# Seven half-size products for eight: the last layer of an attention and MLP kernel by Strassen's method

## The chip, the cores and the metric

The kernel runs on one core of a Trainium2 chip. The metric is the device time of one execution in microseconds (us); the median of several runs is compared. Engines are called PE (TensorE, matmuls), DVE (VectorE), ACT (ScalarE), POOL (GpSimd) and SP (SyncE, which issues transfers).

## The reference

Eight batches of attention with a relative position bias, then an MLP on all 8 x 576 = 4608 rows:

```python
scores = q @ k.T / sqrt(64) + bias           # per batch and head: 576 x 576
attn   = softmax(scores)
x      = (attn @ v), heads side by side      # 4608 x 512
h      = x @ w_in                            # 4608 x 2048
s      = sin(alpha * h)
g      = h + s * s / (alpha + 1e-9)
out    = g @ w_out                           # 4608 x 512
```

## The kernel before

The attention goes batch by batch (t = 0 to 7), the MLP in nine blocks (b = 0 to 8) of 512 rows. All matmuls have f16 operands and write f32 into PSUM, the tile `pb` of eight banks of 512 columns each.

The attention of a batch makes scores (k stationary, q moving, runs of six matmuls of 512 columns), exponentials on ACT into `u`, a multiplication by exp(bias) (`m2r`, `mhr`) on DVE for the part near the diagonal, and attention times v (`av`: nine matmuls of 65 or 130 columns for 128 rows and a pair of heads). DVE divides by the row sums (`rd`, `xn`), and a transposing transfer, or TensorE and a copy, puts the result into `xT`.

A block of the MLP has two stages. `plan_moe_in`: for each of 16 tiles f of 128 hidden columns, four matmuls of 512 columns into a bank `h`; ACT takes the sine, ACT or DVE squares it, and DVE forms g (`gg`), which lies in SBUF as `g[:, f, 512]`, f16. `plan_mo`: for each of the four groups of 128 rows, 16 matmuls of 512 columns (g stationary, `w_out16` moving) add up in one bank; a copy by DVE or ACT into `outs` and a transfer on SP's queue end it. The two banks for these products are 7 and 6 in turn.

The order of each engine's instructions is made when the kernel is built, by `Plan.run`: tasks with a cost per engine, dependencies, a priority and buffers, of which always the one that can start first is emitted. Output products are marked `fill`: they are put between a batch's score runs (`QUOTA` of them at most while the scores run). So the output products of block b mostly run inside the attention of batch b + 1. Engines work in order; the waits between them (semaphores) are put in from the order of emission and from the tiles that instructions touch.

Loads on POOL's queue: `stage_kq(t)` copies k and q of a batch, cast to f16, into DRAM (576 KB each), from where SP's transposing transfers fetch them; `load_v16(t)` loads v. In the kernel before, the first g of block b (1 to 6) triggers `load_v16(b + 1)` and `stage_kq(b + 2)`; a separate task stages batch 2.

Of the kernel before, what the change touches and what calls it, by code (L numbers as in the profile page):

```python
# [13 lines left out]
ALU = mybir.AluOpType  # L14
# [21 lines left out]
NBUF = {"ut": 2, "u": 2, "g": 2, "s16": 3, "sq": 3, "outs": 5, "xn": 6}  # L36
PAIRS = ((0, 1), (2, 3), (4, 5))
BANKS = {"h": (0, 1, 2, 3, 4, 5), "av": (6, 7), "mo": (7, 6)}


class Task:
    def __init__(self, engs, emit, deps, pri, nb=0.0):
        self.engs, self.emit, self.deps, self.pri, self.nb = engs, emit, list(deps), pri, nb
        self.allocs = []
        self.marks = []
        self.offs = None
        self.s_only = self.fill = False
        self.pad = ()
        self.end = self.eng = None
# [12 lines left out]
class Plan:  # L62


    def __init__(self):
        self.tasks = []
        self.sin = self.in_qk = False
# [26 lines left out]
    def pick(self, b, taken):  # L94
        sets = PAIRS if b.tag == "sc" else [(k,) for k in BANKS[b.tag]]
        best = None
        for ks in sets:
            if any(k in taken for k in ks):
                continue
            fr = [self.bank_free(k) for k in ks]  # L100
            if any(x is None for x in fr):
                continue
            if best is None or max(fr) < best[0]:
                best = (max(fr), ks)
        return best

    def ready(self, t):
        r = t.nb
        for d in t.after:
# [6 lines left out]
        n_ring, banks = {}, set()  # L116
        t.got = []
        for i, b in enumerate(t.allocs):
            if b.tag in NBUF:
                ring, n = self.rings[b.tag], NBUF[b.tag]  # L120
                k = n_ring[b.tag] = n_ring.get(b.tag, -1) + 1
                if len(ring) + k >= n:
                    for x in ring[k - n].users:
                        if x.end is None:
                            return None
                        r = max(r, x.end)
                continue
            got = self.pick(b, banks)
            if got is None:
                return None  # L130
            banks.update(got[1])
            t.got.append((b, got[1]))
            r = max(r, got[0] - (t.offs[i] if t.offs else 0.0))
        return r
# [14 lines left out]
    def run(self, t0):  # L149
        free = {e: t0 for e in ("PE", "ACT", "DVE", "POOL", "SP")}  # L150
        todo = list(self.tasks)
        while todo:
# [21 lines left out]
            for e, c in cands.items():  # L174
                if not c:
                    continue
                s0 = min(x[0] for x in c)
                st, t = min(((x[0], x[1]) for x in c if x[0] <= s0 + SLACK[e]),
                            key=lambda x: (x[1].pri, x[0]))
                fin = st + t.engs[e]  # L180
                if best is None or (st, fin) < best[:2]:
                    best = (st, fin, e, t)
# [18 lines left out]
            for x, off in t.marks:  # L201
                x.end, x.eng = st + off + LAT[e], e
# [7 lines left out]
WINDOW = 700  # L210
# [5 lines left out]
SPLIT = {0: 3, 1: 3}  # L216
# [24 lines left out]
SQ = {"ACT": 0.52, "DVE": 0.38}  # L241
# [9 lines left out]
AV_PRI = 400  # L251
# [18 lines left out]
def kernel(  # L270
# [61 lines left out]
    zz = sgl.tile([128, 512], F16, name="zz")  # L332
# [6 lines left out]
    phi_x = sgl.tile([NB, EW + 2 * NB], F16, name="phi_sb")  # L339
    phi_sb, less_last = phi_x[:, 0:EW], phi_x[:, EW : EW + 2 * NB].bitcast(F32)  # L340
    e_sb = sgl.tile([H, EW], F16, name="e_sb")
    alphaN = sgl.tile([NF, 128], F32, name="alphaN")
# [33 lines left out]
    def new_sq():  # L376
        return tp.tile([128, DM], F16, name="sq", tag="sq", bufs=NBUF["sq"])

# [279 lines left out]
    def plan_unit(t, p, kind, c, u, ub, done, gate, base):  # L658
# [73 lines left out]
        elif kind == "A":  # L732
            lo, hi = max(0, 128 * c - 128), min(512, 128 * c + 256)

            def bd(e):
                io = u.v[:, y, 0:8, lo:hi].rearrange("p (z c) q -> p z c q", z=2)[:, :, c]
                x0 = lo - 128 * c + 128
                nc.vector.tensor_tensor(  # L738
                    out=io, in0=io, in1=m2[:, 2 * p : 2 * p + 2, x0 : x0 + hi - lo], op=ALU.mult
                )  # L740

            engs = {"DVE": 0.1 + (hi - lo) / 960.0}
# [60 lines left out]
    def plan_att(t, gates, gate):  # L803
# [5 lines left out]
        runs = (A[0:3], [(0, "C", 0)], A[3:6], A[6:9], A[9:12], [(2, "C", 0)], A[12:15],  # L809
                A[15:] + [(0, "B", 0), (2, "B", 0)], [(0, "X", 0)])  # L810
        bases = [PB + 700 * i for i in range(len(runs))]
        exps, head, seen = [], [], set()
        for i, units in enumerate(runs):
# [18 lines left out]
            tl = plan_tail(t - 1, base) if i == 0 and t > 1 else None  # L832

            def run(e, i=i, made=made, tl=tl, fresh=fresh):
                if i == 0:
                    plan.in_qk, plan.used = True, 0
                    plan.quota = QUOTA1 if t == 1 else QUOTA
# [3 lines left out]
                if i == len(runs) - 1:  # L841
                    plan.in_qk = False
                for x in made:
                    x[2](e)
                if tl:
# [6 lines left out]
                         use=use + ([tl[3]] if tl else []))  # L852
            m.offs = ([d] if tl else []) + [0.0] * len(new) + [
                0.1 + 0.2185 * k - GUARD[x[1]] * (k > 1) for k, x in enumerate(units)]
            m.marks = [(x[1], o) for x, o in zip(made, ends)] + ([(tl[4], d + D_TAIL)] if tl else [])
            head = [m]
            exps += [x[3] for x in made]
        for p in range(NP):
            plan_av(t, [(p, 128 * i) for i in range(3)], *us[p // 2], done, bases[(2, 3, 5, 7)[p]],
                    p < (2, NP - 1)[t > 1])  # L860
# [5 lines left out]
        return exps  # L866
# [22 lines left out]
    def plan_tail(t, base):  # L889
# [23 lines left out]
        def norm(e):  # L913
            xn.v = new_xn()
            norm_av(av.v, xn.v)

        x = plan.add({"DVE": 0.67}, norm, [mark], base, new=[xb], use=[ab])
# [40 lines left out]
    def plan_av(t, parts, u, ub, done, base, dma):  # L958
# [42 lines left out]
        x = plan.add({"DVE": (0.4 if t else 0.29) + 128 * nq / 960.0}, norm, prev, base + (NORM_PRI if t else NORM0),  # L1001
# [42 lines left out]
    def plan_moe_in(b, tbl):  # L1044
# [5 lines left out]
        for f in range(NF):  # L1050
# [3 lines left out]
            def mm(e, js, f=f, h=h, hb=hb):  # L1054
# [4 lines left out]
                for y, a, n in ((0, x0, m), (m, 0, 512 - m)):  # L1059
                    if n == 0:  # L1060
                        continue
                    for j in js:
                        full(h.v[:, y : y + n], w_in16[:, j, 128 * f : 128 * f + 128],
                             xT[:, j, a : a + n], j == 0, j == 3)
# [14 lines left out]
            def gg(e, f=f, h=h, sq=sq):  # L1079
# [12 lines left out]
            pri = PB + 10000 + 1000 * (b - (PB // 1000000)) + 10 * f  # L1092
            nb = T_W[f // 8] if b == 0 else 0.0
            m = None
            if f < SPLIT.get(b, 0):
                m = plan.add({"PE": 3 * t_pe(512)}, lambda e, mm=mm: mm(e, range(NP - 1)), xs[1], pri - PRI_S,
                             nb=nb, new=[hb])
# [3 lines left out]
                         use=[hb] if m else [])  # L1101
# [10 lines left out]
    mo_last = []  # L1112

    def plan_mo(b, a):

        for c0, c1 in ((0, 384), (384, DM)) if (b, a) == (T, 3) else ((0, DM),):
            mb, ob, m = Buf("mo"), Buf("outs"), Cell()
            n = c1 - c0
            for f in range(NF):
# [13 lines left out]
                mo_last[0].fill = True  # L1133

# [8 lines left out]
            y.s_only = True  # L1143

# [11 lines left out]
    for t in range(T):  # L1156
        PB = 1000000 * t

        if t > 0:
            gate = [plan.add({"ACT": D_TBL}, lambda e: set_table(EXP_SET), sins, PB)]  # L1160
        exps = []
        for p in range(NP - 1) if t == 0 else ():
            for kq in range(2):
                tr[(0, p + 1, kq)] = plan_tr(0, p + 1, kq, (150, 650, 5)[p], T_PAIR[p][kq])
        if t == 0:
            for g in range(2):
                exps += plan_att0(g, pe_gate, gate)
        else:
            exps += plan_att(t, pe_gate, gate)
            if t == 1:  # L1170
                exps += plan_late(PB + LATE, gate)
        if t == 0:
# [3 lines left out]
            plan.add({"POOL": 5.0}, lambda e: stage_kq(2), [], 10090,  # L1176
# [4 lines left out]
        def turn_in(e, t=t):  # L1181
            load_kqT(t + 1)
            load_kt(t + 1)

        tbl = [plan.add({"ACT": D_TBL}, swap, exps, PB)]
        if 1 <= t < T - 1:
            plan.add({"SP": 5.5}, turn_in, [], PB + 9000, after=tbl + [
                x for tt, _, _, x in xdone if tt == t and "SP" in x.engs])
# [3 lines left out]
        for b in [t] if t < T - 1 else [t, t + 1]:  # L1192
            m, s_ = plan_moe_in(b, tbl)
            sins += s_
        pe_gate = [m]
        for b in [t] if t < T - 1 else [t, t + 1]:
            for a in range(4):
                plan_mo(b, a)
# [31 lines left out]
```

## Time and profile before

Three runs took 373.75, 372.87 and 376.17 us; the profiled execution spans 374.9 us.

| engine | busy us | share of the span | instructions |
|---|---|---|---|
| PE | 368.2 | 98% | 3576 |
| DVE | 257.8 | 69% | 559 |
| ACT | 315.7 | 84% | 431 |
| POOL | 91.9 | 25% | 133 |

The costliest groups that the change touches, from the list of groups by shape:

| line, engine, what | count | busy us | mean ns |
|---|---|---|---|
| L457 PE output products, 512 columns | 560 | 135.5 | 379 |
| L457 PE first-layer products, 512 columns | 448 | 99.2 | 379 |
| L1082 DVE g, 128x512 | 144 | 101.3 | 744 |
| L1077 DVE sq, 128x512 | 75 | 30.9 | 422 |
| L539 DVE copy of an output, 128x512 | 25 | 17.2 | 686 |
| L953 DVE xn, 128x256 and 128x384 | 29, 28 | 12.3, 15.6 | 425, 557 |
| L738 DVE masked u, 128x512 and 128x768 | 64, 64 | 26.8, 35.9 | 423, 563 |

A middle block takes about 39.55 us from one attention's end to the next (194.96 to 234.51): PE busy 39.55, ACT 36.58, DVE 29.50. A row of a timeline gives start, length, engine, line, output <- inputs, tile size, shape, how many were merged, and in brackets the idle time before it with the engine that ended it. A matmul's length contains its way through the array, so lengths overlap; starts tell the pace.

### The profile page before, as it was taken

To read this page: it belongs to the slowest core of one execution; us is meant where nothing else is said; L and a number is where in the kernel's file an instruction comes from. 1 tells how busy PE (TensorE), PEld (TensorE's weight loads), DVE (VectorE), ACT (ScalarE), POOL (GpSimd) and SP (SyncE) were. 2 spreads that over 40 slices of the span, in tenths; PEclk is the share of its full clock that TensorE was granted. 3 is DMA by queue.
4 is the path that set the end of the run, shared out by engine and by line. 5 is a ranking of instruction groups with operands and counts; after the bars stand their busy time and mean duration, and the time that the engine had idled before them with its cause. 6 is when DMAs were issued, how large, how long until landed. Compare 5 with 4: busy or idle time off the path is not lost.

```text
span 374.9 us, 8925 instructions
## 1 busy us (share of the span) xinstructions
PE 368.2 (98%) x3576; PEld 197.4 (53%) x3576; DVE 257.8 (69%) x559; ACT 315.7 (84%) x431; POOL 91.9 (25%) x133
## 2 busy tenths in 40 slices
PE   8999999999999999999999999999999999999996
PEld 3455454644455455684564455444576455444443
DVE  3496976759676967597758867786759675879000
ACT  2787989979997999899989999799979997999211
POOL 7368270037000640055002800090006000000000
PEclk9999999999999999999999999999999999999999
DMA  9969999369922998199917992699249121000112
GB/s 168 201 113 192 200 173 160 83 112 112 133 64 62 151 143 123 48 160 137 133 48 134 125 168 58 122 88 187 59 111 118 65 58 47 7 27 5 73 69 85
DMA packets 149114, 40.49 MB, mean 108 GB/s; under 512 B 137080, under 2 KB 143568, under 8 KB 149072
## 3 DMA queue, kind: packets, MB, share of 16 engines
q0 software_dynamic: 96032, 17.67, 58.3%
q1 hardware_dynamic: 52864, 22.16, 24.6%
q8 instruction: 28, 0.46, 0.5%
q10 hardware_dynamic: 176, 0.09, 0.1%
q14 instruction: 14, 0.11, 0.1%
HBM read 37.73 MB, written 16.56 MB: 145 GB/s over the span
## 4 chain that ended last, share of the span: by engine, by line
PE 95%; ACT 3%; DVE 1%; issue 0%; ACTq 0%
PE pb L457 92%; ACT u L707 3%; PE pb L556 2%; PE pb L1024 1%; PE pb L550 0%; DVE xn L953 0%; DVE u L738 0%; DVE qT L539 0%; DVE zz L508 0%; ACT outs L537 0%; ACT xT L537 0%; DVE rd L952 0%; PE pb L646 0%; PE pb L934 0%; ACTq L537 0%
## 5 line engine op out<-in xcount | busy, mean ns | idle before, releaser
L707 ACT ACTIVATE u<-pb 128x1024 f16<-128x1024 f32 (+1 forms) x146 | 137.4, 1017 | 11.9 <-PE pb L457 10.5
L457 PE MATMUL pb<-w_out,g 128*128 128x512 f16 (+2 forms) x592 | 139.0, 374 | 0.0
L457 PE MATMUL pb<-xT,w_in 128*128 128x512 f16 (+4 forms) x704 | 127.4, 340 | 0.0
L1082 DVE SCALAR_TENSOR_TENSOR g<-sq,inv_a,pb 128x512 f16<-128x512 f16 x144 | 101.3, 744 | 7.1 <-PE pb L457 2.7
L1068 ACT ACTIVATE s<-pb,alphaT 128x512 f16<-128x512 f32 x144 | 92.9, 692 | 12.4 <-PE pb L457 11.9
L457 PEld LDWEIGHTS <-w_in 128*128 128x128 f16 x704 | 64.6, 98 | 57.4
L457 PEld LDWEIGHTS <-g 128*128 128x128 f16 x592 | 53.9, 98 | 60.2 <-issue 5.6
L738 DVE TENSOR_TENSOR u<-u,m2r 128x512 f16<-128x512 f16 (+1 forms) x128 | 62.3, 493 | 33.6 <-ACT u L707 31.9
L457 PEld LDWEIGHTS <-u 128*128 128x128 f16 x1152 | 43.4, 97 | 9.6 <-issue 4.6
L402 POOL COPY kt<-kT 64x256 f16<-64x256 f16 x12 | 4.9, 410 | 172.0 <-DMA kT<-staged_k 107.8
L457 PE MATMUL pb<-qT,kT 64*128 64x64 f16 (+1 forms) x512 | 43.3, 293 | 1.1 <-ACT u L707 0.6
L1075 ACT ACTIVATE sq<-s 128x512 f16<-128x512 f16 x69 | 43.1, 637 | 1.2 <-DVE g L1082 0.3
L457 PE MATMUL pb<-v,u 128*128 128x65 f16 x1024 | 43.7, 193 | 0.0
L1077 DVE TENSOR_TENSOR sq<-s 128x512 f16<-128x512 f16 x75 | 30.9, 422 | 12.5 <-ACT s L1068 11.7
L953 DVE TENSOR_TENSOR xn<-pb,rd 128x256 f16<-128x256 f32 (+2 forms) x59 | 28.5, 483 | 2.0
L457 PEld LDWEIGHTS <-kT 64*128 64x128 f16 x512 | 16.2, 95 | 23.1 <-issue 16.8
L457 PE MATMUL pb<-vh,u 128*128 128x130 f16 x128 | 28.2, 221 | 0.0
L407 POOL DMA_DIRECT2D v<-in_v_dram x28 | 24.8, 900 | 4.0 <-DMA nat<-in_k_dram 2.1
L537 ACT ACTIVATE outs<-pb 128x512 f32<-128x512 f32 (+2 forms) x12 | 6.9, 572 | 19.9 <-PE pb L457 19.9
L952 DVE RECIPROCAL rd<-pb 128x4 f32<-128x4 f32 (+2 forms) x59 | 11.0, 186 | 13.3 <-PE pb L457 13.1
L539 DVE COPY outs<-pb 128x512 f32<-128x512 f32 x25 | 17.2, 686 | 4.1 <-PE pb L457 4.1
L1146 ACT ACT_TABLE_LOAD x15 | 19.2, 1283 | 0.3
(75 smaller groups left out, 192.5 us busy)
## 6 DMA issues: line engine op xcount, KB each, us to landing
out_dram<-outs SPq DMA_DIRECT2D x35, 256.0 KB, 2.8
v<-in_v_dram POOLq DMA_DIRECT2D x28, 128.0 KB, 4.6
staged_k<-in_k_dram POOLq DMA_DIRECT2D x6, 576.0 KB, 8.9
staged_q<-in_q_dram POOLq DMA_DIRECT2D x6, 576.0 KB, 12.1
w_in<-in_moe_w_in_dram POOLq DMA_DIRECT2D x4, 512.0 KB, 8.5
w_out<-in_moe_w_out_dram POOLq DMA_DIRECT2D x4, 512.0 KB, 14.5
w_out<-in_v_dram SPq DMA_DIRECT2D x6, 128.0 KB, 5.7
xT<-xn SPq DMA_TRANSPOSE x47, 2.4
```

The costliest lines, as they stand in the source:

```text
L407: nc.gpsimd.dma_start(out=vs[t % 2][:, c, :, 0:D], in_=vp[128 * c : 128 * c + 128],)
L457: nc.tensor.matmul(out=out, lhsT=lhsT, rhs=rhs, start=start, stop=stop)
L539: k_of(e).tensor_copy(out=o, in_=i)
L707: nc.scalar.activation(out=o, in_=x, func=AF.Exp, scale=0.125)
L738: nc.vector.tensor_tensor(out=io, in0=io, in1=m2[:, 2 * p : 2 * p + 2, x0 : x0 + hi - lo], op=ALU.mult)
L952: nc.vector.reciprocal(out=r, in_=x[:, :, :, D])
L953: nc.vector.tensor_tensor(out=xn[:, 0:n].rearrange("p c (z d) -> p c z d", z=2), in0=x[:, :, :, 0:D], in1=r.unsqueeze(3).to_broadcast([128 ...
L1068: nc.scalar.activation(out=s16.v, in_=h.v, func=AF.Sin, scale=alphaT[:, f : f + 1])
L1075: nc.scalar.activation(out=sq.v, in_=s16.v, func=AF.Square)
L1077: k_of(e).tensor_tensor(out=sq.v, in0=s16.v, in1=s16.v, op=ALU.mult)
L1082: nc.vector.scalar_tensor_tensor(out=gcell[b].v[:, f, :], in0=sq.v, scalar=inv_a[:, f : f + 1], in1=h.v, op0=ALU.mult, op1=ALU.add,)
L1146: nc.scalar.preload_act_table_set(name)
```

## The change

Blocks 1 to 8 make `out = g @ w_out` by Strassen's method (Winograd's form). g of a block is cut in two by rows (256 each) and in two by hidden columns (even and odd tiles f), `w_out` in two by hidden columns and in two by output columns. Seven products of 256 x 1024 x 256 are made instead of eight, from quarters or from sums of quarters: S1 to S4 of g (per block, eight DVE instructions of 1024 elements) and sums of w_out (once, 16 DVE instructions, three new tiles `wt` and one in place of a quarter of `w_out16`). Each product's two row halves (c = 0, 1; 8 matmuls of 256 columns each) lie side by side in one bank, and each half is copied or added out of it: 4 copies and 10 adds per block. Block 0 stays as it was.

Besides: products may fill all of a batch's score stage (`plan.quota` 1000); `SPLIT` lets the first three quarters of the first two sines' products start early in blocks 2 to 7; the tail (rows 512 to 575 of the batch before) goes with the second run of scores instead of the first; the last `av` of batches 4 to 7 is cut in two; priorities of `av` and constants of the planner change; small tables share memory with `wt`. Score stages may go before other work (`qk`), and blocks can be grouped (`GROUPS`), but each group here has one batch. `stage_kq` is now driven by `stage_at`.

The diff, cut to its core:

```diff
-BANKS = {"h": (0, 1, 2, 3, 4, 5), "av": (6, 7), "mo": (7, 6)}
+BANKS = {"h": (0, 1, 2, 3, 4, 5), "av": (6, 7), "mo": (7, 6), "mw": (7,)}
...
+GROUPS = ([0], [1], [2], [3], [4], [5], [6], [7])
...
-SPLIT = {0: 3, 1: 3}
+SPLIT = {0: 3, 1: 3, **{b: 2 for b in range(2, 8)}}
...
-AV_PRI = 400
+AV_PRI = 800
...
-            tl = plan_tail(t - 1, base) if i == 0 and t > 1 else None
+            tl = plan_tail(t - 1, base) if i == TAIL_RUN and t > 1 else None
...
-                if f == 0 and 1 <= b < T - 1:
+                if f == 0 and (b in v_at or b in stage_at):
                     nc.gpsimd.tensor_copy(out=tick, in_=gcell[b].v[0:1, 0, 0:1])
-                    load_v16(b + 1)
-                    if b + 2 < T:
-                        stage_kq(b + 2)
+                    for x in v_at.get(b, ()):
+                        load_v16(x)
+                    for x in stage_at.get(b, ()):
+                        stage_kq(x)
...
+    slots = Buf("mw"), {}, Cell()
+
+    def plan_mo_w(b):
...
+            x = s_task("S3", j, n, lambda fs=fs: (A(0, 0, fs), A(0, 1, fs)), lambda fs=fs: s3[:, fs],
+                       ALU.subtract, own + ([made[("S3", 0)]] if j else []),
+                       [] if j else [b3], [gb, b3] if j else [gb])
...
+        bb, ends, mo = slots
...
+        def prod(i, k, fresh):
+
+            lhs, rhs, need, src = prods[k]
+            for c in range(2):
+                cs = slice(256 * c, 256 * c + 256)
+                for f in range(0, 8, 2):
+
+                    def mm(e, f=f, c=c, cs=cs):
+                        if b == 1 and i + c + f == 0:
+                            mo.v = bank(bb)
+                        for ff in (f, f + 1):
+                            nc.tensor.matmul(
+                                out=mo.v[:, cs], lhsT=lhs(ff, c), rhs=rhs(ff),
+                                start=fresh and ff + c == 0, stop=ff == 7,
+                                skip_group_check=not fresh or c == 1)
...
+        def c_op(k, name, other, c, rows=None, col=None):
...
+                if other is None:
+                    copy_on(e, o, mo.v[:, cs])
+                else:
+                    nc.vector.tensor_tensor(out=o, in0=tiles[other][0].v[:, cs], in1=mo.v[:, cs], op=ALU.add)
...
+        block(0, 1, True, "a", None)
+        block(1, 2, False, "C11", None, 0, 0)
...
+        block(2, 6, True, "x", "a")
+        block(3, 5, True, "y", "x")
+        block(4, 7, True, "C22", "y", 1, 1)
+        block(5, 4, False, "C21", "x", 1, 0)
+        block(6, 3, True, "C12", "y", 0, 1)
...
+    for x in range(2, T):
+        if of[x - 1] < of[x]:
+            v_at.setdefault(x - 1, []).append(x)
+        else:
+            v_tail.add(x - 2)
+        stage_at.setdefault(GROUPS[max(0, of[x] - 2)][-1], []).append(x)
...
+            def stages(e):
+                for x in stage_at[0]:
+                    stage_kq(x)
```

`block` emits one product and takes its two halves out (`prod`, then `c_op` twice). In the changed kernel the output product's matmuls are at line 1292, the adds at 1320, copies at 572 (DVE) and 570 (ACT), the S sums at 1235, the sums over w_out at 1203.

More of the change, by code (lines that the diff above doesn't have):

```diff
@@ L96, in pick @@
         best = None
+        if b.tag == "mo" and self.one_mo and any(
+                self.held[k] is not None and self.held[k].tag == "mo" and self.bank_free(k) is None
+                for k in BANKS["mo"]):
+            return None
         for ks in sets:
@@ L116, in ready @@
         n_ring, banks = {}, set()
+        soft = 0.0
         t.got = []
@@ L176, in run @@
                     continue
+                if e == "PE":
+                    q = min((x[0] for x in c if x[1].qk), default=None)
+                    if q is not None and q < free[e] + QK_WAIT:
+                        c = [x for x in c if x[1].qk or max(x[0], free[e]) + x[1].engs[e] <= q + QK_TOL]
                 s0 = min(x[0] for x in c)
@@ L200, in run @@
             t.end, t.eng = fin + LAT[e], e
-            for x, off in t.marks:
-                x.end, x.eng = st + off + LAT[e], e
+            late = max(0.0, t.stall - st)
+            for i, (x, off) in enumerate(t.marks):
+                x.end, x.eng = st + off + (late if t.soft and i >= t.soft_mark else 0.0) + LAT[e], e
             free[e] = fin
@@ L207, in run @@
         self.made = max(free.values())
-WINDOW = 700
+WINDOW = 900
+T_WT = 50.0
+SG = 4
+SOFT = (1,)
+LAST = True
+GROUPS = ([0], [1], [2], [3], [4], [5], [6], [7])
+S_ONLY = True
+PS = 10900
+QK_WAIT = 0.0
+QK_TOL = 0.1
+R0 = 3
+TAIL_RUN = 1
 WARM_END = 22.0
@@ L240 @@
 NORM0 = 1200
-SQ = {"ACT": 0.52, "DVE": 0.38}
+SQ = {"ACT": 0.52, "DVE": 0.35}
 T_V = ((15.5, 19.0), (50.0, 50.0))
@@ L331 @@
         "p (h c d) -> p h c d", h=H, c=4)
-    zz = sgl.tile([128, 512], F16, name="zz")
+    wt = [sgl.tile([128, 8, 256], F16, name=f"wt{i}") for i in range(3)]
+    half = {k: sgl.tile([128, 8, 256], F16, name=f"half{k}") for k in (2, 3)}
+    hd = wt[0].rearrange("p f n -> p (f n)")
+    zz = hd[:, 0:512]
     tick = sgl.tile([1, 1], F16, name="tick")
@@ L855, in plan_att @@
             m.marks = [(x[1], o) for x, o in zip(made, ends)] + ([(tl[4], d + D_TAIL)] if tl else [])
+            n0 = (1 if tl else 0) + len(new)
+            if len(units) > 2 and t in SOFT:
+                m.soft, m.soft_mark = set(range(n0 + 2, n0 + len(units))), 2
             head = [m]
@@ L858, in plan_att @@
         for p in range(NP):
-            plan_av(t, [(p, 128 * i) for i in range(3)], *us[p // 2], done, bases[(2, 3, 5, 7)[p]],
-                    p < (2, NP - 1)[t > 1])
+            cut = 1 if t >= 6 else 2
+            for part in (range(cut), range(cut, 3)) if LAST and p == NP - 1 and t > 3 else (range(3),):
+                plan_av(t, [(p, 128 * i) for i in part], *us[p // 2], done, bases[(2, 3, 5, 7)[p]] + 100 * part[0],
+                        p < (2, NP - 1)[t > 1] or part[0] > 0)
         for g in range(2):
@@ L915, in norm @@
             norm_av(av.v, xn.v)
-        x = plan.add({"DVE": 0.67}, norm, [mark], base, new=[xb], use=[ab])
+            if t in v_tail:
+                nc.gpsimd.tensor_copy(out=tick, in_=xn.v[0:1, 0, 0:1])
+                load_v16(t + 2)
+        x = plan.add({"DVE": 0.57}, norm, [mark], base, new=[xb], use=[ab])
         x0 = S * t % XN + 512
@@ L1062, in mm @@
                     for j in js:
-                        full(h.v[:, y : y + n], w_in16[:, j, 128 * f : 128 * f + 128],
-                             xT[:, j, a : a + n], j == 0, j == 3)
+                        nc.tensor.matmul(
+                            out=h.v[:, y : y + n], lhsT=w_in16[:, j, 128 * f : 128 * f + 128],
+                            rhs=xT[:, j, a : a + n], start=j == 0 and y == 0, stop=j == 3,
+                            skip_group_check=y > 0)
             def sn(e, f=f, h=h, s16=s16):
@@ L1112 @@
     mo_last = []
+    mo_of = {b: [None] * NF for b in range(T + 1)}
     def plan_mo(b, a):
@@ L1143, in plan_mo, with plan_wt, sub, f @@
             y.s_only = True
+    wdone = {}
+    def plan_wt():
+        w = w_out16.rearrange("p (f z) n -> p z f n", z=2)
+        def sub(o, a, b, deps, pri, nb=T_WT):
+            def f(e):
+                k_of(e).tensor_tensor(out=o, in0=a, in1=b, op=ALU.subtract)
+            n = o.shape[1] * 256
+            return plan.add({"DVE": 0.08 + n * 0.00052}, f, deps, pri, nb=nb)
+        for j in range(0, 8, 2):
+            fs = slice(j, j + 2)
+            b11, b12 = w[:, 0, fs, 0:256], w[:, 0, fs, 256:512]
+            b21, b22 = w[:, 1, fs, 0:256], w[:, 1, fs, 256:512]
+            pri = PB + 500 + j
+            x1 = sub(wt[0][:, fs], b12, b11, [], pri)
+            x3 = sub(wt[2][:, fs], b22, b12, [], pri)
+            x2 = sub(wt[1][:, fs], b22, wt[0][:, fs], [x1], pri)
+            x4 = sub(b12, b21, wt[1][:, fs], [x2, x3] + mo_of[0][2 * j : 2 * j + 4], pri)
+            for f in range(j, j + 2):
+                wdone[f] = {5: x1, 6: x2, 7: x3, 4: x4}
@@ L1191 @@
         sins = []
[L1192 to L1193 removed]
+        blocks = grp if t < T - 1 else grp + [T]
+        for b in blocks:
+            m, s_ = plan_moe_in(b, tbl, PB + 10000 + 1000 * blocks.index(b), head if t > 1 else [])
             sins += s_
         pe_gate = [m]
[L1196 to L1198 removed]
+        for b in blocks:
+            if b == 0:
+                for a in range(4):
+                    plan_mo(b, a)
+                plan_wt()
+            else:
+                plan_mo_w(b)
     plan.run(T_START)
```

186 lines of the change are left out of this document (147 added, 39 removed).

## The prediction

> **What bounds the kernel now.** I read the page's busy shares first, then the clock in its slices, then the chain that ended last.
>
> ```profile
> PE 368.2 (98%) x3576; PEld 197.4 (53%) x3576; DVE 257.8 (69%) x559; ACT 315.7 (84%) x431; POOL 91.9 (25%) x133
> ...
> PEclk9999999999999999999999999999999999999999
> ...
> PE 95%; ACT 3%; DVE 1%; issue 0%; ACTq 0%
> ```
>
> TensorE (PE) is busy throughout at full clock and 95% of the chain is its work: matmul time taken away comes off the end, and every new TensorE wait is added to it. The timeline of TensorE in a middle block gives real pitches:
>
> ```profile
> 195.57 0.38 PE L457 MATMUL pb<-w_out,g 128*128 128x512 f16 x1
> 195.78 13.98 PE L457 MATMUL pb<-xT,w_in 128*128 128x512 f16 x64
> 209.59 2.97 PE L457 MATMUL pb<-w_out,g 128*128 128x512 f16 x13
> ```
>
> 64 matmuls of 512 columns start within 209.59 - 195.78 = 13.81 us, 0.2158 us each, though a row calls one 0.38 long: a matmul's end lies some 0.165 us behind its last column, which the next one hides and a waiting engine does not. The period of a block, from one such group to the next (235.33), is 39.55 us; in it VectorE (DVE) is busy 29.5 and ScalarE (ACT) 36.6.
>
> Then a place where TensorE hands a PSUM tile to VectorE and waits for it (timeline, all engines):
>
> ```profile
> 30.41 0.54 PE L457 MATMUL pb<-v,u 128*128 128x65 f16 x10
> ...
> 30.98 0.18 DVE L952 RECIPROCAL rd<-pb 128x4 f32<-128x4 f32 x1
> ...
> 31.19 0.42 DVE L953 TENSOR_TENSOR xn<-pb,rd 128x256 f16<-128x256 f32 x1
> ...
> 31.67 0.28 PE L1024 MATMUL pb<-id_sb,xn 128*128 128x128 f16 x2 [0.71 <-DVE xn L953]
> ```
>
> The last of ten 65-column matmuls starts at 30.95 - 0.193 (its row's mean) = 30.76. VectorE starts at 30.98, 0.22 later; less 0.027 for 65 columns that is 0.195 us behind the last column. xn ends at 31.61 and TensorE goes on at 31.67: 0.06 us.
>
> **The change, part by part.** *Fewer columns.* A block's output product is now 7 x 16 matmuls of 256 columns instead of 64 of 512. A group of nine attention matmuls (one of 130, eight of 65 columns: 650) starts 0.30 us after the one before it. With 512a + b = 0.2158 and 650a + 9b = 0.30, a column takes 0.415 ns and each matmul 0.003 us on top; the weight loads, 98 ns long by their rows, are hidden even at 65 columns. A 256-column matmul is then 0.1095 us, and a block 112 x 0.1095 = 12.26 against 13.81: 1.55 saved, 12.4 us in eight blocks. Six transposes fewer save 6 x 0.057 = 0.3.
>
> *New sums on VectorE.* By back-to-back starts in the timeline g takes 0.66 us, sq 0.35, a masked u of 768 elements 0.48 and of 512 0.36, a 512-column copy 0.61. An S sum of 1024 f16 elements extrapolates to 0.60 (0.12 per 256 more), an add of 256 columns from PSUM lies near xn of 256 (0.36 to 0.42), a 256-column copy at 0.34. By the built order a middle block loses four copies (2.4) and about one sq, and gains 8 S (4.8), 10 adds (3.7) and 4 copies (1.4): VectorE goes from 28.2 to about 36 us per block. That fits beside TensorE's 38 to 41, so I price it at nothing; if the sums ran at xn's pace per element, they would cost 8 x 0.55 more (rival two). The 16 sums over w_out, 5.6 us once, lie where block 1's attention leaves VectorE idle.
>
> *One bank.* Before, output products alternate between two PSUM banks, each read only when complete. Now all seven use bank 7, the two row halves (c) side by side in it, and the instruction that takes a half out (line 1320, or a copy) stands in the order after the first two to six matmuls of the next half. In the built order the waits show what this means. TensorE, block 4, product 6 (the first half's matmuls are 4690 to 4704):
>
> ```
> 4700 L1292 Matmult pb<-wt_81,half_83 128x256
> 4702 L1292 Matmult pb<-wt_81,half_83 128x256 [waits DVE_49]
> ```
>
> The semaphore value awaited at 4702 is that of VectorE's copy of the half before; that copy waits for 4700, not only for its own last matmul. So the two take turns on the bank: TensorE stops inside a half until VectorE has read the other one. What is queued behind 4702 is everything TensorE has, score and attention matmuls too. Price of one turn: 0.107 + 0.195 until VectorE starts, 0.42 to 0.48 for the add (xn 256 is 0.425; g of 512 less 256 columns is 0.477; I take 0.425, the nearer shape), 0.06 back: 0.79, less the 0.1095 that the matmul took anyway: 0.68 us. Bounds: 0.61 (0.36, xn's back-to-back start) to 0.73 (0.477).
>
> Where other TensorE work of at least that length lies between, it is hidden: a run of six score matmuls (216.47 to 217.23, 0.76 us) just covers it, a group of attention matmuls (0.9) does. Going through the 112 turns of the built order, 60 have nothing between: 7 in block 1, then 5, 6, 4, 5, 5 in blocks 2 to 6, and all 14 of block 7 and of block 8, where only products are left. Eight of these 28 are ScalarE's copies, about as long (128x256, 0.38). Three turns of block 1 and 5 are partly covered, 0.4 together. Sum: 60 x 0.68 + 0.4 = 41.2 us; bounds 37 to 44.
>
> [...]
>
> *A second staging.* The first g of block 0 now also stages block 2's k and q, and the task `stages` does it again: seven pairs on GpSimd's (POOL) queue where there were six. The first pair stands ahead of block 1's v and vh loads.
>
> ```profile
> 60.51 0.22 PE L457 MATMUL pb<-vh,u 128*128 128x130 f16 x1
> ```
>
> This is the first matmul that needs them. By the DMA answers the last vh was issued at 47.4 and landed 9.7 us later, at 57.1; the staging, issued behind it at 50.7 and 52.8, landed at 60.8 and 64.6. The transfers land one after another, so the pair takes 7.5 us; put ahead, vh lands at 64.6. TensorE reaches that matmul at about 60.6 in the new order (one score run and three products more ahead, six products fewer before). It waits 4.0 us; bounds 0 (if transfers shared the queue) to 5. The kt copies behind the loads come at 53 to 55.6, when first used: under 0.5 more. Later pairs wait for nothing TensorE needs: block 2's k lands about 72, its scores start after 90.
>
> *The rest.* SPLIT, tail and AV in parts reorder work that TensorE has anyway; first-sine products ahead hide waits that the chain does not contain, so nothing is gained. Attention is left with bank 6 alone (7 is held), but six score matmuls or more lie between its groups. The last output is a 256-column add (0.43) instead of a 128-column ScalarE copy (0.28): +0.15.
>
> **Sum.** The profiled execution spans 374.9 us, 1.1 above the 373.75 median of the three runs (372.87 to 376.17). 374.9 - 12.4 - 0.3 + 41.2 + 4.0 + 0.15 = 407.5 in a profile; less 1.1, 406 us as a median. Middle blocks go from 39.55 to 39.55 - 1.55 + 5 x 0.68 = 41.4 us; after block 8's last first-layer matmul each half takes 8 x 0.1095 + 0.68 = 1.56 us instead of 0.88.
>
> **The rivals.** One, the other side: the halves overlap, the waits being satisfied when TensorE gets there. For it: the planner prices the taking out as free of TensorE, and where score runs lie between it is. Then the time is 374.9 - 12.7 + 4.0 + 0.15 - 1.1 = 365. It decides below (12.7 - 4.15) / 60 = 0.14 us per turn. Against it: 0.195 us pass before VectorE even starts. [...]
>
> Two: VectorE becomes the bound as well. S sums read g in strides of two tiles; at the pace of xn, (557 - 425) / 128 = 1.03 ns per element, one takes 0.36 + 0.79 = 1.15 us. VectorE then needs 36 + 4.4 = 40.4 of a block's 41.4; if it can be filled no further than ScalarE is now (36.6 of 39.55, 93%), the period is 43.4, 2 us more in six blocks, and 1 in the tail: 406 + 13 = 419. Against it: masked u, strided f16 too, goes at (563 - 423) / 256 = 0.55 ns per element. 0.10.
>
> Three: half the turns' price is absorbed, since in the planned order TensorE has waits of its own (ScalarE is busy 36.6 of 38.0 us of an ideal period) that the turns only replace. 406 - 20 = 386. For it: three engines above 90%; against it: the tail's 28 turns have nothing to replace. 0.08.
>
> **How the numbers follow.** The forecast keeps 0.75; its own range is 398 (0.61 per turn, no wait for vh) to 411 (0.73 per turn, 5 us). Eight in ten: 391 to 419 reaches to rival two and half-way to three, leaving out rival one and most of three. A measurement here tells 1% (3.7 us) from no change. Faster by over 1% is rival one's 0.07; within 1% 0.02, where rival one and half-price turns meet; slower the other 0.91.
>
> **What would show it.** Matmuls L1292 idle before <- VectorE L1320 and the copies, some 60 times at about 0.5 us (0.68 less the hidden tail of the matmul); TensorE's share falling to about 90%; 1.56 us per half at the end; seven staged pairs, and one wait of about 4 us before vh,u near 60 us; S sums at 0.70 us per row. Wrong if L1292 starts every 0.11 us across halves at the end, or if g or u on VectorE are what TensorE waits for.

## The result, and the profile after

The changed kernel takes 413.15 us (median of 4 runs, 411.49 to 416.39), the kernel before 374.49 in the runs beside it: a ratio of 1.107, 95% interval 1.100 to 1.113 (the quotient of the two medians is 1.103). The forecast was 406, range 391 to 419. The profiled execution spans 411.9 us. From its page, the lines that answer to those of before (busy times, granted clock by slice, chain):

```profile
PE 364.1 (88%) x3940; PEld 230.9 (56%) x3940; DVE 321.3 (78%) x721; ACT 314.0 (76%) x436; POOL 96.6 (23%) x136
...
PEclk9999998999999999999999999999999999999999
...
PE 76%; DMA 9%; DVE 8%; ACT 3%; issue 2%; POOL 1%; SPq 0%; DVEq 0%
```

TensorE is busy 4.1 us less and the span is 37 us longer: it waits. (It loses more than 4.1 us of matmul time, but each wait lays bare the end of the matmul before it, which counts as busy: 0.165 us by the prediction's rows, 10 us in 62 waits.) VectorE is no longer 1% of the chain but 8%, and DMA, which was not in it, 9%. One slice of the granted clock shows 8. Which waits, says the view of TensorE's waits (engine, what waited, for what; us in total, times, longest):

```profile
PE pb L1292 <- DVE outs L1320: 16.4, 32, 0.5
PE pb L1292 <- DVE sn L1320: 8.1, 15, 0.8
PE pb L490 <- DMA vh<-in_v_dram: 4.0, 1, 4.0
PE pb L1292 <- DVE outs L572: 2.6, 5, 0.5
PE pb L1292 <- ACT outs L570: 1.9, 4, 0.5
PE pb L1292 <- ACT sn L570: 1.9, 4, 0.5
PE pb L1108 <- DMA xT<-xn: 1.9, 1, 1.9
PE pb L490 <- ACT u L740: 1.6, 5, 0.5
...
PE pb L1292 <- DVE sn L572: 1.0, 2, 0.5
```

Six of these rows are output products (L1292) that wait until a half has been read out of the bank: 62 times, 31.9 us, 0.51 each. How one such turn looks at the end of the kernel, where there is nothing else to do, is in the timeline:

```profile
379.66 0.42 DVE L1320 TENSOR_TENSOR outs<-sn,pb 128x256 f32<-128x256 f32 x1 [1.12 <-PE pb L1292]
380.14 0.81 PE L1292 MATMUL pb<-wt,half 128*128 128x256 f16 x6 [0.51 <-DVE outs L1320]
380.79 0.38 PE L1292 MATMUL pb<-w_out,g 128*128 128x256 f16 x2
381.21 0.42 DVE L1320 TENSOR_TENSOR outs<-sn,pb 128x256 f32<-128x256 f32 x1 [1.12 <-PE pb L1292]
381.68 1.25 PE L1292 MATMUL pb<-w_out,g 128*128 128x256 f16 x10 [0.51 <-DVE outs L1320]
```

Two matmuls of the next product start (380.79), TensorE stops, VectorE adds (381.21), TensorE goes on 0.05 us after its end. It is a semaphore that it waits for, put in when the kernel is built; what the chip would do without it, no run shows. From stop to stop 1.54 us pass for eight matmuls of 0.11. And the place where v's last rows are needed:

```profile
58.34 0.38 PE L490 MATMUL pb<-w_out,g 128*128 128x512 f16 x1
62.70 0.23 PE L490 MATMUL pb<-vh,u 128*128 128x130 f16 x1 [3.99 <-DMA vh<-in_v_dram]
...
64.40 1.46 PE L490 MATMUL pb<-qT,kT 64*128 64x512 f16 x6
```

After the 4 us of idle time the six score matmuls take 1.46 us; undisturbed such a run takes 0.82 (a row of the first experiment). The view by windows puts the granted clock of 60 to 70 us at 0.83.

One run of this kernel can be some 4 us longer or shorter than another by what TensorE does in its first 20 us; the last section shows it.

### The profile page after: what moved, and what is told of

Read it like the earlier page. It is cut to its first block, busy times and chain, and to the rows that moved or that the text cites. A ratio compares the mean times of both kernels' runs of the same rounds, so it can differ in the third digit from the quotient of the medians.

```text
span 411.9 us, 9836 instructions
## 1 busy us (share of the span) xinstructions
PE 364.1 (88%) x3940; PEld 230.9 (56%) x3940; DVE 321.3 (78%) x721; ACT 314.0 (76%) x436; POOL 96.6 (23%) x136
## 4 chain that ended last, share of the span: by engine, by line
PE 76%; DMA 9%; DVE 8%; ACT 3%; issue 2%; POOL 1%; SPq 0%; DVEq 0%
PE pb L1108 27%; PE pb L1292 27%; PE pb L490 22%; DMA w_out<-in_moe_w_out_dram 5%; DVE outs L1320 4%; DMA vh<-in_v_dram 3%; ACT u L740 2%; DVE sn L1320 2%; DVE u L771 1%; DMA xT<-xn 1%; DVE outs L572 1%; POOL w_out L476 1%; POOL nat L465 0%; ACT sn L570 0%; ACT outs L570 0%
## 5 line engine op out<-in xcount | busy, mean ns | idle before, releaser
L1108 PE MATMUL pb<-xT,w_in 128*128 128x512 f16 (+4 forms) x704 | 129.0, 340 | 1.9 <-DMA xT<-xn 1.9
L1292 PE MATMUL pb<-w_out,g 128*128 128x256 f16 x512 | 69.0, 272 | 19.3 <-DVE outs L1320 14.3
L1292 PEld LDWEIGHTS <-g 128*128 128x128 f16 x640 | 59.3, 97 | 45.6 <-issue 36.0
L771 DVE TENSOR_TENSOR u<-u,m2r 128x512 f16<-128x512 f16 (+1 forms) x128 | 59.3, 489 | 5.5 <-ACT u L740 4.3
L490 PEld LDWEIGHTS <-u 128*128 128x128 f16 x1152 | 44.8, 98 | 10.2 <-DMA vh<-in_v_dram 4.3
L1122 ACT ACTIVATE sq<-s 128x512 f16<-128x512 f16 x79 | 48.7, 635 | 0.3
L1292 PE MATMUL pb<-wt,half 128*128 128x256 f16 x256 | 36.6, 272 | 10.1 <-DVE sn L1320 5.0
L1320 DVE TENSOR_TENSOR outs<-sn,pb 128x256 f32<-128x256 f32 x48 | 20.2, 420 | 21.4 <-PE pb L1292 21.2
L1292 PEld LDWEIGHTS <-half 128*128 128x128 f16 x256 | 23.7, 97 | 19.1 <-issue 16.6
L1124 DVE TENSOR_TENSOR sq<-s 128x512 f16<-128x512 f16 x65 | 27.0, 421 | 6.4 <-ACT s L1115 6.3
L490 PEld LDWEIGHTS <-kT 64*128 64x128 f16 x512 | 14.9, 95 | 19.2 <-issue 12.4
L997 DVE RECIPROCAL rd<-pb 128x4 f32<-128x4 f32 (+2 forms) x63 | 11.5, 182 | 18.1 <-PE pb L490 17.7
## 6 DMA issues: line engine op xcount, KB each, us to landing
staged_q<-in_q_dram POOLq DMA_DIRECT2D x7, 576.0 KB, 11.7
```

The costliest lines, as they stand in the source:

```text
L490: nc.tensor.matmul(out=out, lhsT=lhsT, rhs=rhs, start=start, stop=stop)
L771: nc.vector.tensor_tensor(out=io, in0=io, in1=m2[:, 2 * p : 2 * p + 2, x0 : x0 + hi - lo], op=ALU.mult)
L1108: nc.tensor.matmul(out=h.v[:, y : y + n], lhsT=w_in16[:, j, 128 * f : 128 * f + 128], rhs=xT[:, j, a : a + n], start=j == 0 and y == 0, st ...
L1122: nc.scalar.activation(out=sq.v, in_=s16.v, func=AF.Square)
L1124: k_of(e).tensor_tensor(out=sq.v, in0=s16.v, in1=s16.v, op=ALU.mult)
L1292: nc.tensor.matmul(out=mo.v[:, cs], lhsT=lhs(ff, c), rhs=rhs(ff), start=fresh and ff + c == 0, stop=ff == 7, skip_group_check=not fresh or ...
```

## The experiments

**One staging (e1).** Block 0's first g stages nothing.

```diff
-                    for x in stage_at.get(b, ()):
+                    for x in stage_at.get(b, ()) if b else ():
                         stage_kq(x)
```

> The changed kernel with block 2's k and q staged once, as before the change: the first g of block 0 triggers no staging. Theory (the second pair stands ahead of the v loads on GpSimd's queue): the one wait of 4.0 us for vh near 59 us goes, and if the low granted clock between 60 and 70 us (mean 0.83, worth some 1.7 us) follows from that idle time, it goes too: 413.15 - 5.7 = 407.5 us. If the clock dips there for a reason of its own, 409. Rival: another wait (kt, exponentials on ScalarE) ends last at the same place: 412 to 413.

Measured: 411.56 us (407.08 to 413.32), ratio 1.099 (1.092 to 1.105): the interval overlaps that of the changed kernel, so the time alone decides nothing. The timeline of this kernel's TensorE does:

```profile
62.79 0.38 PE L490 MATMUL pb<-w_out,g 128*128 128x512 f16 x1
63.01 0.22 PE L490 MATMUL pb<-vh,u 128*128 128x130 f16 x1
...
64.00 0.82 PE L490 MATMUL pb<-qT,kT 64*128 64x512 f16 x6
```

No wait for vh, no half pace; the granted clock of 60 to 70 us is 1.00. This profiled execution, the longest of the four, began slowly: its last transposes before block 1's attention start at 49.01 us instead of 45.03. The next long run of first-layer matmuls starts at 77.57 instead of 78.19. So 4.6 us were gained in between, against 5.7 expected; a wait for w_out grew from 0.54 to 1.02. The low clock (0.83) goes with the wait of 3.99 us and is gone with it, so between these two profiles it is its consequence and has no reason of its own.

**Two banks in the last two blocks (e2).**

```diff
+T2 = 7
...
+        pair = b >= T2
...
-                cs = slice(256 * c, 256 * c + 256)
+                sep = pair and c == 1
+                buf, cell = two if sep else (bb, mo)
+                cs = slice(0, 256) if sep else slice(256 * c, 256 * c + 256)
```

> The changed kernel, but in blocks 7 and 8 the second row half (c = 1) of each product has PSUM bank 6, free by then, and only c = 0 has bank 7; all engines' order stays. Theory (TensorE and the reader take turns on one bank): 28 turns of about 0.67 us go, 413.15 - 18.8 = 394.5 us, and each half after the last first-layer matmul takes 0.875 us instead of 1.55. If VectorE (32.4 busy of 37 us between 335 and 372) then holds block 7's part, only block 8's 14 turns are gained: 403.5. Rival (turns replace waits that come anyway, for the same adds further on): under 4 us gained, 410 or more.

Measured: 397.7 us (395.37 to 400.56), ratio 1.067 (1.060 to 1.074). From the timeline of TensorE:

```profile
375.75 7.19 PE L1297 MATMUL pb<-w_out,g 128*128 128x256 f16 x64
382.77 1.91 PE L1297 MATMUL pb<-wt,half 128*128 128x256 f16 x16
384.52 1.91 PE L1297 MATMUL pb<-wt,g 128*128 128x256 f16 x16
```

No stop between halves: 16 matmuls in 1.75 us, and 64 start within 7.02, 0.1097 each. The waits for readings fall from 62 to 35; 27 turns of 0.67 are 18.1 us, and the span falls by 17.1, with the granted clock of 60 to 70 us lower this time (0.66). The median falls by 15.5, against 18.8 expected. All engines do the same work in the same order as in the changed kernel: the bank alone makes the difference.

**Every add twice (e3).**

```diff
-                    nc.vector.tensor_tensor(out=o, ...)
+                    for _ in range(2):
+                        nc.vector.tensor_tensor(out=o, ...)
```

> The changed kernel with every add of a half (line 1320) done twice by VectorE, the same result written twice; the order is otherwise the same. Theory of the turns: TensorE waits for the reading, so every add that has no other TensorE work beside it costs its 0.42 us again, and those whose cover is 0.8 us long begin to cost: by the built order the adds' part goes from 33.9 to 62.3 us, 413 + 28 = 441 us (bounds 433 to 446). Rival (half of the turns' price stands in place of waits that TensorE has anyway): the second half is absorbed too, 420 to 427. Rival (TensorE does not wait for the adds): 413 to 416.

Measured: 460.36 us in a single run, 47 more. The two rows of waits for adds:

```profile
PE pb L1292 <- DVE outs L1321: 33.4, 37, 1.4
PE pb L1292 <- DVE sn L1321: 17.6, 24, 1.3
```

51.0 us instead of 24.5: 26.5 more, where 28 were expected; next to nothing of it is absorbed. The other 20 were in no one's expectation. The view by windows, near the end (stretch, length, busy time of PE, PEld, DVE, ACT, POOL, granted clock):

```profile
430.00:440.00 10.00, 5.99 (x35) 3.94 (x34) 3.37 (x8) 0.00 (x0) 0.00 (x0) 0.70 0.04 14
440.00:450.00 10.00, 6.83 (x30) 4.11 (x29) 2.75 (x7) 0.00 (x0) 0.00 (x0) 0.50 0.12 41
```

With waits of 0.97 us in every half the granted clock falls to a half, and the matmuls between them take nearly twice as long: the page's row of granted clocks, in slices of 11.5 us, has 9 from 390 to 401 us and then 8, 5, 7, 5 and 5, and a row of eight matmuls lasts 1.87 us (at 445.04) where one of the changed kernel lasts 1.03. By the page the output matmuls from `w_out` and g last 299 ns in the mean (512 of them) and those from `wt` and the half sums 281 (256 of them), both 272 in the changed kernel: 16 us more in all, the largest part of the 20; 14 more waits than in the changed kernel lay bare 0.165 us each (2.3, an estimate), and block 1's attention started 1.8 later.

**The S2 and S3 sums twice (e4).**

```diff
-                k_of(e).tensor_tensor(out=o, in0=x, in1=y, op=op)
+                for _ in range(2 if name in ("S2", "S3") else 1):
+                    k_of(e).tensor_tensor(out=o, in0=x, in1=y, op=op)
```

> The changed kernel with the S2 and S3 sums done twice by VectorE (the same result written twice): 4 more instructions of 0.69 us per block, 22 us of VectorE time in all. Theory (VectorE is no bound, the sums lie beside TensorE's work): 413 to 417 us, the excess only where an add of a half queues behind a sum. Rival (VectorE bounds the middle blocks, busy 36 of some 43 us): most of it comes onto the time, 428 to 435.

Measured: 429.4 us in a single run, 16.3 more: as the rival said. Of TensorE's waits, the rows that grew:

```profile
PE pb L1293 <- DVE outs L1321: 19.8, 32, 2.1
PE pb L1293 <- DVE outs L572: 8.9, 10, 2.2
...
PE pb L1293 <- DVE sn L572: 4.8, 4, 1.7
```

Together 33.5 instead of 20.0 us, 13.5 of the 16.3. The readings queue behind the sums on VectorE, up to 2.2 us instead of 0.5. In the changed kernel no such wait is longer than 0.8 us, so the sums cost little there; but what hides them is used up, and 22 us more would not fit.

**The kernel before, profiled again (e5).**

> The kernel before, profiled once more. In its first profile six transposes of 96 columns at 5 us took 0.69 us and TensorE's matmuls stayed at about half pace until some 20 us; in the changed kernel's profile the same six took 0.42 us and the attention stood 4 us earlier at 45 us. If that pace is a matter of the single execution, this profile may show 0.42 and a span near 371 us; if it belongs to the kernel, 0.69 and 375 us again.

Measured: 375.05 us, span 373.1. The second six transposes, first in the earlier profile, then in this one:

```profile
6.96 0.66 PE L550 MATMUL pb<-id_sb,natx 96*128 96x96 f16 x6
```

```profile
6.71 0.43 PE L550 MATMUL pb<-id_sb,natx 96*128 96x96 f16 x6
```

It is a matter of the execution, not of the kernel. This one was at half pace again from 18 to 23 us (granted clock 0.85 from 20 to 30), so its span is only 1.8 us shorter.

**One reading per product (e6).** Still one bank; a product's 512 columns are read at once.

```diff
-            for c in range(2):
-                c_op(k, name, other, c, rows, col)
+            c_op(k, name, other, 1, rows, col)
...
-            cs = slice(256 * c, 256 * c + 256)
+            cs = slice(0, 512)
```

> The changed kernel, all products still in bank 7, but each product is read out once, 512 columns, after both row halves, instead of twice 256 columns: 56 turns instead of 112. Theory (each turn has a fixed part, the way to the reader and back, and a part by columns): a turn is dearer, about 0.107 + 0.195 + 0.69 + 0.06 - 0.11 = 0.94 us, but by the built order 32 are uncovered instead of 60 and some covers are too short by 0.2: 30 + 5.6 = 36 us against 41, so 408 us. Rival (the price goes by the columns read, not by turns): 62 x 256 columns are still waited for, 412 to 415. Rival (less VectorE time in fewer instructions is what matters, 4 copies of 0.34 and 10 adds of 0.42 become 7 of about 0.69): also near 413.

Measured: 409.26 us (408.83 to 409.42), ratio 1.093 (1.087 to 1.098); 408 was expected. From its timeline:

```profile
382.59 1.91 PE L1292 MATMUL pb<-w_out,g 128*128 128x256 f16 x16 [1.22 <-DVE outs L1320]
...
384.53 0.69 DVE L1320 TENSOR_TENSOR outs<-sn,pb 128x512 f32<-128x512 f32 x1 [0.67 <-PE pb L1292]
385.27 1.91 PE L1292 MATMUL pb<-w_out,g 128*128 128x256 f16 x16 [0.78 <-DVE outs L1320]
```

From 382.59 to 385.27 are 2.68 us for 16 matmuls of 0.1097: the turn costs 0.92, forecast 0.94. Where the add stood behind an S sum it is dearer (1.22 of waiting). Now 41 waits make 29.9 us, with 0.165 of bared matmul for each 36.7; 36 was expected, and the changed kernel has 41.9.

**Two banks throughout (e7).**

```diff
-    slots = Buf("mw"), {}, Cell()
...
+            mb, mo = Buf("mo"), Cell()
...
-        block(4, 7, True, "C22", "y", 1, 1)
-        block(5, 4, False, "C21", "x", 1, 0)
-        block(6, 3, True, "C12", "y", 0, 1)
+        block(4, 7, ("C22", "y", 1, 1), ("z", "x", None, None))
+        block(5, 3, ("C12", "y", 0, 1))
+        block(6, 4, ("C21", "z", 1, 0))
```

> The changed kernel with each product in a bank of its own, 7 and 6 in turn and shared with attention times v as before the change; it is read out once, 512 columns, while the next product is made in the other bank. The two sums that grew inside one bank are made by VectorE from the readings instead (one copy becomes an add, one add more per block). Everything else stays, the second staging too. Theory (the turns are the loss): TensorE's waits for readings go, 62 x 0.67 = 41.5 us: 413.15 - 41.5 = 371.5 us. Rival (VectorE, busy 36 us of a block that would last 38.5, then bounds the middle blocks): 376 to 385. Rival (the loss lies elsewhere): above 400.

Measured: 380.86 us (379.64 to 383.32), ratio 1.018 (1.011 to 1.024). Of the loss of 38.7 us 32 are gone. The first rows of its waits:

```profile
PE pb L490 <- DMA vh<-in_v_dram: 3.4, 1, 3.4
PE pb L490 <- DMA qT<-staged_q: 2.2, 1, 2.2
PE pb L490 <- ACT u L740: 2.1, 5, 0.5
PE pb L1291 <- DVE outs L1312: 1.3, 4, 0.3
```

The waits for readings are 1.3 us in all; 371.5 us was the forecast, so 9 us are lost elsewhere. That the time lies where the rival had it (376 to 385) is not yet that VectorE is the reason; transfers stand first.

**Two banks, one staging, the tail rows earlier (e8).**

```diff
-TAIL_RUN = 1
+TAIL_RUN = 0
...
-                    for x in stage_at.get(b, ()):
+                    for x in stage_at.get(b, ()) if b else ():
```

> The kernel of e7 with block 2's k and q staged once, and the tail rows again with the first run of scores, as in the kernel before. Theory: the wait for vh (4.0 us) and the low clock behind it (1.7 us) go: 371.5 - 5.7 = 366 us, below the kernel before (373.0). Rival (VectorE bounds the middle blocks): 371 to 380, no better than before.

Measured: 378.35 us (376.48 to 379.92), ratio 1.012 (1.005 to 1.018), 12 above the forecast. The vh wait is gone, and TensorE now waits twice for the fetching of q, 6.0 us in all (in e7 once, 2.2), the longer time again with half pace behind it (six matmuls in 1.47 us):

```profile
254.29 1.47 PE L490 MATMUL pb<-qT,kT 64*128 64x512 f16 x6 [3.57 <-DMA qT<-staged_q]
```

**The staging later (e9, e10).** Two kernels, the staging set off by the ninth and by the fourteenth g.

```diff
-                if f == 0 and (b in v_at or b in stage_at):
-                    nc.gpsimd.tensor_copy(out=tick, in_=gcell[b].v[0:1, 0, 0:1])
+                if f == 0 and b in v_at or f == F_ST and b and b in stage_at:
+                    nc.gpsimd.tensor_copy(out=tick, in_=gcell[b].v[0:1, f, 0:1])
...
```

> The kernel of e8, with the staging of k and q (GpSimd's queue) set off by the ninth g of a block instead of the first, some 7 us later; the loads of v stay with the first. In e8 TensorE waits twice, 3.6 and 2.4 us, for q's transposing transfer, which runs from 242.6 to 254.3 us beside v's loads and the staging (issued from 237 to 246 us). Theory (they share the DMA engines): these 6.0 us go, 378.35 - 6.0 = 372.4 us, level with the kernel before (373.7) or 1 us below. Rival (the transfer waits for its place on SyncE's queue): 378. Rival (VectorE, busy 318 of 374 us, then holds the same place): 375 to 377.

> As e9, with the staging set off by the fourteenth g of a block, some 5 us later again, when the next batch's k and q have been fetched. Theory (shared DMA engines): as e9, 372.4 us, or up to 1 us less if part of the collision was left. Rival (staged data then come late for the batch after): a new wait for kT or qT, 376 or more.

Measured: 372.5 us (ratio 0.997, 0.995 to 0.9995) and 371.8 us (0.9956, 0.992 to 0.999). The wait for q falls from 6.0 to 2.4 and 2.1 us; TensorE, VectorE and ScalarE have the same order in all three kernels, so the staging beside q's transfer was the cause of that part. It was not the whole: the transfer behind the longer wait of e8 took 11.7 us from issue to landing (242.6 to 254.3), in the last kernel 9.0 (241.5 to 250.5), in e5 4.9 (238.1 to 243.0). What still slows it, v's loads or its place among SyncE's transfers, is not shown. The last kernel takes 0.4% less time than the kernel before; compared with the profile of e5, TensorE is busy 11.8 us less (352.8 against 364.6) and idle 8 us more.

**What keeps the rest? (e11, e12)** Once VectorE is relieved in that last kernel, once ScalarE loaded.

```diff
+                if b > 1:
+                    o, x, y = o[:, 0:1], x[:, 0:1], y[:, 0:1]
                 k_of(e).tensor_tensor(out=o, in0=x, in1=y, op=op)
```

> The kernel of e10, but from block 2 on each S sum is made over a quarter of its elements only (256 of 1024), so that most of S1 to S4 is left out and the products are made from what lies there; the order of all engines stays. VectorE does some 56 x 0.40 = 22 us less (from 0.69 for 1024 elements at 0.52 ns each). In e10 the middle blocks last 39.7 us, as before the change, though TensorE needs only 38.0. Theory (VectorE, busy 36 of 40 us, is what keeps them there): blocks fall to 38, 371.8 - 9 = 363 us. Rival (ScalarE, 36.5 of 40, or the fetching of k and q keeps them): 370 to 372.

This kernel leaves out three quarters of each S sum from block 2 on, so its output is not the product; only its time is of use. Measured: 371.29 us, ratio 0.993 (0.990 to 0.996), though the sums took 0.284 us instead of 0.684 each and VectorE was busy 20 us less (298.4 against 318.8). The theory falls: VectorE does not keep the blocks of this kernel.

```diff
-                    nc.scalar.activation(out=sq.v, in_=s16.v, func=AF.Square)
+                    for _ in range(2 if f % 3 == 0 else 1):
+                        nc.scalar.activation(out=sq.v, in_=s16.v, func=AF.Square)
```

> The kernel of e10 with 26 of ScalarE's 78 squares done twice (the same result written twice), 26 x 0.635 = 16.5 us more for ScalarE, some 2 us in a block. If ScalarE keeps the blocks at 39.7 us, most of it comes onto the time: 383 to 388. If it has 3 us of slack in each, as its busy time says, 372 to 376.

Measured: 378.84 us, ratio 1.013 (1.008 to 1.018): 7 of 16.5 us come onto the time, between the two cases (by the profile ScalarE is busy 14.8 us more, 325.7 against 310.9). ScalarE has slack, but less than its busy time says. Of the last kernel's named TensorE waits after 75 us, 5.5 us in all, most are for q (2.1), xT (1.0) and readings, sums and norms on VectorE (2.4); the exponentials cost 2.4 before, 1.9 of it in block 1's attention. That these are the whole of the missing 8 us is not shown.

## Why the prediction was right, and where it was short

*Fewer columns, 12.4 us:* right. 0.1095 us was forecast for a 256-column matmul, 0.1097 is the pace in e2.

*One bank, 41.2 us:* right, in mechanism, place, count and price: 62 waits of 0.51 us for 60 of about 0.5, at most one more in a block than forecast, 1.54 us per half at the end for 1.56, and e2 gives 0.63 us of span for each of the 27 turns that go. In the rows of the end above no reading overlaps a matmul on bank 7: the add runs from 381.21 to 381.63 us, the matmuls before it end at 381.17 and the next start at 381.68. Rival one (365), the overlapping halves, did not occur: 413.15 was measured.

*VectorE at nothing:* right for the changed kernel, by a thin margin. A sum takes 0.684 us (row forecast 0.70), not the 1.15 of rival two; but e4 shows that rival's mechanism at 2.8 us more per block, with 16 us on the time. It is not "busy share near 93%" that decides (in e4's blocks 4 to 6 VectorE is busy 38.8 of 44.7 us, 87%), but that the readings stand behind the sums in one queue, while TensorE stands behind the readings.

*Half absorbed (rival three):* next to nothing is. Doubled adds came onto TensorE's waits at 26.5 of 28 us.

*A second staging, 4.0 us:* the wait is 3.99 us, with two errors that cancelled: vh landed at 62.66 instead of 64.6 and TensorE was there at 58.7 instead of 60.6. Missing was what the idle time does to the clock: 0.17 of 10 us, 1.7 us.

*The starting point:* the sum went from the profile of 374.9, called 1.1 above the median. But that is a span, and a run's time is 1.7 to 2.1 us longer than its span (413.68 for 411.9), so that run was some 3 us above the median; that 1.1 served as well is luck, the two differences nearly cancel. e5 shows why it was above: the first 20 us of that profile ran at half pace; the changed kernel's did not. So the profiles are compared from one place on, the first short scores of block 1's attention (in the kernel before less 0.65 us for three output products that stand ahead of them there):

```profile
50.53 0.64 PE L457 MATMUL pb<-qT,kT 64*128 64x64 f16 x32
```

```profile
45.41 0.64 PE L490 MATMUL pb<-qT,kT 64*128 64x64 f16 x32
```

From there to the end the kernel before takes 325.0 us in both of its profiles (in e5 the place is at 48.74), the changed one 366.5: 41.5 more, where the sum had 32.6 (the medians, with all sorts of starts, differ by 38.7). From the same place the kernel of e7 takes 332.1, so two banks took away 34.4 of the 41.5, and that of e10 323.5, 1.5 less than the kernel before. The step that was short is the last one of the working, the rest, which was priced at nothing but 0.15: 62 turns of 0.675 instead of the 41.2 (0.7), the clock after vh (1.7), waits for g (0.6), for w_out in block 0's products (0.5), for exponentials (1.2, none in e5 behind this place), for kt (0.2), 0.165 us of bared matmul at each of nine such waits (1.5, an estimate), and this (the chain of waits: start, length, what):

```profile
202.11 0.43 DVE outs L1320
...
202.56 0.38 SPq L1327
...
202.99 4.10 DMA xT<-xn
...
207.13 0.38 PE pb L1108
```

An output's transfer on SyncE's queue waits for a reading, and behind it stands the transposing transfer of xT, for which TensorE then waits 1.9 us. The prediction asked who is queued behind a waiting TensorE, not who is queued behind the transfer that a late reading lets go. This is read from the chain; no run tests it. With it the list makes 8.3 us for a gap of 8.9.

## What to carry to other kernels

An arithmetic saving on the busiest engine has to be set against what it costs to get the results out: count the hand-overs per accumulator, ask of each whether other work of the writer stands between, and price the uncovered ones as way there, reading, way back. Where a reader and a writer share a bank and a semaphore keeps them apart, the writer stops at each reading that no other work covers (62 of 112 here, 0.51 us each); a second bank gave back 17 us in two blocks here with nothing else changed (e2), and two banks in turn, with whole products read at once and two sums of a block moved from the bank to VectorE, 32 of 39 us (e7). And when a change lets an engine arrive earlier, every transfer that used to be in time has to be looked at again.

## What the hardware showed besides

In one run the granted clock fell during regular short waits, in others after a long one. 0.51 us of waiting in every 1.54 left it at 0.99 (372 to 412 us of the changed kernel). In e3 it was 0.97 in every 2.0 or so (an estimate: 1.54 and 0.46 more of waiting): the page's row has 9 from 390 to 401 us and then 8, 5, 7, 5 and 5 to the end, with 0.50 from 440 to 450, and the output matmuls of that run last 16 us more in all. Of the single waits, the 4.0 us before vh in the changed kernel were followed by 0.83 (60 to 70 us), the 3.6 us before q in e8 by six matmuls in 1.47 us instead of 0.82; the other wait for q in e8, 2.4 us, left the page's row at 9. Two waits of 3.4 us before vh differ: in e6 the row stays at 9 throughout, in e7 it has a 7 from 67 to 76 us, where a row of two matmuls of 512 columns lasts 1.06 us instead of 0.59. What decides between one pattern and the other, these runs do not tell.

In the first 20 us one program ran in two ways: the same six transposes in 0.66 and 0.43 us. In the changed kernel and e1, alike up to there, this moved the start of block 1's attention from 45.41 to 49.38 us, 1% of the time, while the page's row of granted clocks showed 9 in the first two slices of both. Two profiles that are to be compared to 1% have to be compared at their first 20 us as well.
